# Memory columns on one engine, side evacuation one step earlier, and another order of the last projections in a segment-recurrent attention kernel

## The chip, the cores and the metric

One core of one Trainium2 chip. The metric is the device time of one execution in microseconds (us), lower is better. Before the change it was 822.22 us, the median of three runs (822.06 to 823.05). All runs told here were in the fast state; the granted TensorE clock was 0.996 to 1.000 in every one, so the clock explains none of the differences.

## The reference, cut to what matters

The input is one sequence of 2048 rows of 512. It is cut into 64 segments of 32 rows. Each segment is attended to together with 8 memory rows, and the memory of the next segment is the output of this one:

```python
mem = mem0
for s in range(n_seg):                                  # 64 segments
    h = jnp.concatenate([mem, xs], axis=1)              # 8 memory rows + 32 rows of x
    q, k, v = (einsum('btd,dhe->bhte', h, W) for W in (Wq, Wk, Wv))   # 32 heads of 128
    p = softmax(where(mask, q @ k.T * scale, -1e9))
    o = einsum('bhte,hed->btd', p @ v, Wo)
    mem = o[:, :M, :]                                   # recurrence
    outs.append(o[:, M:, :])
out = g * concat(outs) + (1 - g) * mlp(layernorm(x))
```
(written shorter than the original; the weights and the data are bfloat16.)

Only the 8 memory rows are needed to go on to the next segment. The kernel therefore takes "memory columns" out first, and does the output columns of a segment one or two steps later, beside the chain of the memory.

## The kernel before

One iteration of the loop is called a step; `s` is its number and `si = s % 4` its place in a tile of four. `bank(k)` is one of eight PSUM banks. A "side" job is work that isn't in the recurrence (keys, queries and values of the eight rows of a segment that don't fit beside the memory in a tile of 32 columns, and the output projection); it is done in small pieces where TensorE has room. Its copy out of PSUM is put in a queue and done by `flush`:

```python
def later(q, ev, k):            # queue a copy out of side bank k
    side_todo.add(k); q.append((k, ev))

def side(shape, dtype=FP32):    # hand out a side bank: whoever asks may have to empty it first
    side_n[0] += 1
    n = pools["nside"]
    while side_n[0] - n in side_todo:
        flush(dve_q)
        flush(act_q)
    return bank(5 + side_n[0] % n, shape, dtype)

def left_v(T, vb):              # V of the eight other rows: four matmul units, then
    ...
    def ev():
        vt = pools["sb"].tile([P, 4, Dh], BF16, tag="vt", bufs=1, name="vt")
        nc.scalar.copy(out=..., in_=bk[:])              # L282 in the profiles
        nc.sync.dma_start(vds[T][...], vt[...])         # L285, to DRAM and back to change the layout
    later(act_q, ev, side_k)
```

The loop, cut:

```python
for s in range(nseg):
    fill = side_work(T, si)
    ...
    if s >= 2:
        ux_out(s - 2)                     # output columns of two steps ago
        flush(act_q)
    ...
    flush(dve_q)
    for bi, (t, h0, h1) in enumerate(BANKS):            # q and k of the segment (L211),
        ...                                             # transposed on VectorE (L217), cast to QT, KT
    ...                                                 # V (L222), scores, exp
    nc.vector.reciprocal(out=R[...], in_=sm[:])         # L692, softmax sums of the memory rows
    ...                                                 # Pm = E * R (L695)
    Um = [bank(k, [P, NG, 8]) for k in (nd, ne, na, nc_)]
    av(Um, 8, s, V, Pm, 8, 0, 0)                        # P.V of the memory rows (L398, L403)
    sums(sr, ...)                                       # softmax sums of the other rows (L360)
    for j in range(4):                                  # the memory columns (L703)
        (nc.scalar.copy if j % 2 else nc.vector.tensor_copy)(out=UTT[Tp % 2][:, :, j, ...], in_=Um[j][:])
    nc.vector.reciprocal(out=R[:, 8 * NG:]..., in_=sr)  # L704, 1.76 us
    run_fill(1)
    flush(act_q, 2)
    for u in range(8):
        wo_unit(wp, UTT[Tp % 2], 24 - 8 * sp, u)        # Wo of the memory rows (L233); j = 0 first
    nc.scalar.copy(out=wsb[:], in_=wp[:])               # L711
    S_next = mask_mm()                                  # L374, in the bank of the sums
    if s >= 1:
        av_x(s - 1, ...)
    mem_out(aT, wsb)                                    # 16 small matmuls that turn the memory (L365)
    nc.vector.tensor_copy(out=hn[:, :, 0:M], in_=aT)    # hT, the next step's input (L721)
```

The four head groups j = 0 to 3 are copied by VectorE, ScalarE, VectorE, ScalarE. The tail after the last step does the output columns of the last three segments:

```python
    nc.gpsimd.tensor_tensor(out=racc[...], in0=racc[...], in1=Rl, op=ALU.add)
    ...
    wo_x(s - 2, nb, U1, 16)                             # matmuls and copy in one call
    ...                                                 # copies of U of step s - 1
    for _ in out_units(NT - 2):                         # output of the last but one tile
        flush(dve_q, 9)
    av_x(s, (nd, ne, na, nc_))
    wo_x(s - 1, nb, U1, 8)
    ...                                                 # copies of U of step s
    wo_x(s, 6, U0, 0)
    ...                                                 # projection of the left columns in two halves
    o_sb = cw.tile([P, Dm], BF16, tag="o", bufs=1, name="o")   # the same single buffer as in out_units
    for half in range(2):
        ...
        nc.vector.scalar_tensor_tensor(out=o_sb[:, d], ...)
        nc.sync.dma_start(out2[...], o_sb[:, d])
```

Of the kernel before, what the change touches and what calls it, by code (L numbers as in the profile page):

```python
# [11 lines left out]
ALU = mybir.AluOpType  # L12
# [11 lines left out]
def kernel(ctx, tc, A_x, A_mem0, A_Wq, A_Wk, A_Wv, A_Wo, A_seg_len, B_x, B_w1, B_b1, B_w2, B_b2, gate_w, out):  # L24
    nc = tc.nc
    P = 128
    _, S, Dm = A_x.shape
    H, Dh = A_Wq.shape[1], A_Wq.shape[2]
    M = A_mem0.shape[1]
# [5 lines left out]
    NT = S // P  # L35
# [3 lines left out]
    NG = H // 4  # L39
# [116 lines left out]
    for hh in range(4):  # L156
        for g in range(4):
            q = slice(32 * g, 32 * g + 32)
            for (c0, c1) in ((0, M), (EW - LEFT, EW)):
                sl = MkA[q, hh, c0:c1]  # L160
                nc.gpsimd.affine_select(out=sl, in_=sl, pattern=[[0, c1 - c0]], compare_op=ALU.is_ge,
                                        fill=MASK_NEG, base=-LEFT * hh, channel_multiplier=1)
            sl = MkA[q, hh, 0:M]
            nc.gpsimd.affine_select(out=sl, in_=sl, pattern=[[0, M]], compare_op=ALU.is_ge,
                                    fill=MASK_NEG, base=LEFT * hh + LEFT - 1, channel_multiplier=-1)
# [3 lines left out]
                                    fill=MASK_NEG, base=LEFT * hh, channel_multiplier=-1)  # L169
# [3 lines left out]
                                    fill=MASK_NEG, base=M, channel_multiplier=-1)  # L173
# [4 lines left out]
    def bank(k, shape, dtype=FP32):  # L178
        return pools["ps"].tile(shape, dtype, tag=f"b{k}", name=f"b{k}")

    side_n, side_todo = [0], set()
    dve_q, act_q = [], []

    def flush(q, n=1):
        for _ in range(min(n, len(q))):
            k, ev = q.pop(0)
            ev()
            side_todo.discard(k)

    def later(q, ev, k):  # L190
        side_todo.add(k)
        q.append((k, ev))

    def side(shape, dtype=FP32):
# [6 lines that stand above are left out]
# [29 lines left out]
    def wo_unit(bk, ut, c0, u, d0=0, d1=Dm):  # L230
        for (j, i) in HORD[4 * u:4 * u + 4]:
            g = i % 4
            nc.tensor.matmul(bk[32 * g:32 * g + 32, :], lhsT=ut[:, i, j, c0:c0 + 32], rhs=Wo_sb[:, 4 * i + j, d0:d1],  # L233
                             start=(j == 0 and i < 4), stop=(j == 3 and i >= NG - 4), tile_position=(0, 32 * g))
# [81 lines left out]
    def out_units(T):  # L316
        ob = side([P, Dm])
        side_k = side_n[0]
        for si in range(SPT):
            nc.tensor.matmul(ob[32 * si:32 * si + 32, :], lhsT=SelX[:], rhs=wsbs.pop(SPT * T + si + 2)[:], start=True, stop=False,  # L320
                             tile_position=(0, 32 * si))
        yield
        for si in range(SPT):
            nc.tensor.matmul(ob[32 * si:32 * si + 32, :], lhsT=SelL[si][:], rhs=wsbLs[T][:], start=False, stop=True,
                             tile_position=(0, 32 * si))

        def ev():
            o_sb = cw.tile([P, Dm], BF16, tag="o", bufs=1, name="o")
            nc.vector.scalar_tensor_tensor(out=o_sb[:], in0=ob[:], scalar=g_all[:, T:T + 1], in1=c_all[:, T, :], op0=ALU.mult, op1=ALU.add)
            nc.sync.dma_start(out2[T * P:(T + 1) * P, :], o_sb[:])  # L330
        later(dve_q, ev, side_k)
        yield

    def side_work(T, si):


        if si < 3 and T + 1 < NT:
            for n in range(2):
                if si == 0:
                    yield from left_v(T + 1, n)  # L340
                else:
                    yield from left_qk(T + 1, n, si - 1)
        if si == 3 and T >= 2:
            yield from out_units(T - 2)
        if si == 3 and T >= 1:
            yield from wo_left(T - 1)
# [45 lines left out]
    def av(U, n, s, V, Pt, c_main, c_left, u0):  # L392

        T, si = divmod(s, SPT)
        for i in range(NG):
            for j in range(4):
                q = slice(32 * j, 32 * j + 32)
                nc.tensor.matmul(U[j][:, i, :], lhsT=V[q, i, :], rhs=Pt[q, i, c_main:c_main + n],  # L398
                                 start=(i == 0), stop=False, skip_group_check=True, tile_position=(32 * j, 0))
        for g in range(2):  # L400
            for j in range(4):
                q = slice(32 * j, 32 * j + 32)
                nc.tensor.matmul(U[j][:, g:NG:2, u0:u0 + 8], lhsT=VL[T % 2][q, si, g, :], rhs=Pt[q, g:NG:2, c_left:c_left + 8],  # L403
                                 start=False, stop=True, skip_group_check=True, tile_position=(32 * j, 0))
# [188 lines left out]
    UTT = [lp.tile([P, NG, 4, 64], BF16, name=f"UTT{i}") for i in range(2)]  # L593
    racc = lp.tile([P, NG * 40], FP32)
# [15 lines left out]
    fill = iter(())  # L610
# [14 lines left out]
    def av_x(s, banks):  # L625
        U = [bank(k, [P, NG, 32]) for k in banks]
        av(U, 32, s, Vs.pop(s), Pxs.pop(s), 0, 32, 24)
        Uxs[s] = U
# [7 lines left out]
    for s in range(nseg):  # L636
# [3 lines left out]
        fill = side_work(T, si)  # L640
# [7 lines left out]
        na, nb, nc_, nd, ne = ring  # L648
        ring = (nb, nd, ne, na, nc_)
        qk_banks = (na, nb, nc_, nd, ne)  # L650
        if s >= 2:
            ux_out(s - 2)
            flush(act_q)
        if s + 1 < nseg:
            prep_h(s + 1)
        if s >= 1:
# [39 lines left out]
        Um = [bank(k, [P, NG, 8]) for k in (nd, ne, na, nc_)]  # L696
# [3 lines left out]
        sums(sr[:, :, 24:32], E[:, :, 48:56], False, True)  # L700
        Tp, sp = divmod(s - 2, SPT)
        for j in range(4):
            (nc.scalar.copy if j % 2 else nc.vector.tensor_copy)(out=UTT[Tp % 2][:, :, j, 24 - 8 * sp:24 - 8 * sp + M], in_=Um[j][:])  # L703
        nc.vector.reciprocal(out=R[:, 8 * NG:].rearrange("p (i q) -> p i q", q=32), in_=sr)  # L704
        run_fill(1)
        flush(act_q, 2)
# [1 line left out]
        wp = bank(nb, [P, Dm])  # L708
# [22 lines left out]
    Rl = R[:, 8 * NG:]  # L731
# [2 lines left out]
    Px = cw.tile([P, NG, 40], BF16, tag="Px", name="Px")  # L734
    nc.vector.tensor_tensor(out=Px[:, :, 0:32], in0=E[:, :, 16:48], in1=Rq, op=ALU.mult)
    nc.vector.tensor_tensor(out=Px[:, :, 32:40], in0=E[:, :, 48:56], in1=Rq[:, :, 24:32], op=ALU.mult)
    nc.gpsimd.tensor_tensor(out=racc[:, 8 * NG:], in0=racc[:, 8 * NG:], in1=Rl, op=ALU.add)
    Es.pop(s), Rs.pop(s)
    Pxs[s] = Px
    for _ in fill:  # L740
        pass
    flush(act_q, 9)

    def wo_x(sw, k, ut, c0):
        wp = bank(k, [P, Dm])
        for u in range(8):
            wo_unit(wp, ut, c0, u)
        wsb = cw.tile([P, Dm], BF16, tag="wsb", bufs=9, name="wsb")
        nc.scalar.copy(out=wsb[:], in_=wp[:])
        wsbs[sw + 2] = wsb  # L750

    U1, U0 = UTT[(NT - 1) % 2], UTT[NT % 2]
    wo_x(s - 2, nb, U1, 16)
    for j, U in enumerate(Uxs.pop(s - 1)):
        (nc.vector.tensor_copy if j % 2 else nc.scalar.copy)(out=U1[:, :, j, 8 + M:48], in_=U[:])
    for _ in out_units(NT - 2):
        flush(dve_q, 9)
    av_x(s, (nd, ne, na, nc_))
    wo_x(s - 1, nb, U1, 8)

    Ul = Uxs.pop(s)
    for j, U in enumerate(Ul):
        (nc.vector.tensor_copy if j % 2 else nc.scalar.copy)(out=U0[:, :, j, M:32], in_=U[:, :, 0:RIDE])  # L763
    for j, U in enumerate(Ul):
        (nc.vector.tensor_copy if j % 2 else nc.scalar.copy)(out=U1[:, :, j, 32:40], in_=U[:, :, RIDE:32])
    wo_x(s, 6, U0, 0)
    T = NT - 1
    HD2 = Dm // 2
    wL = cw.tile([P, Dm], BF16, tag="wsbL", bufs=1, name="wsbL")
    for half in range(2):  # L770
        d = slice(HD2 * half, HD2 * half + HD2)
        wp = bank((nc_, nd)[half], [P, HD2])
# [35 lines left out]
    with tc.If(n_bad > 0):  # L808
        with tc.tile_pool(name="gp", bufs=1) as gp, tc.tile_pool(name="gps", bufs=2, space=PSUM) as gps:
# [4 lines left out]
            def mem_tr():  # L814
                mp = gps.tile([P, KC, M], BF16, tag="m", name="mp")
                for kc in range(KC):
# [7 lines left out]
                                    fill=MASK_NEG, base=-M, channel_multiplier=1)  # L824
# [98 lines left out]
```

## Time and profile before

| what | before |
|---|---|
| time, median of 3 runs | 822.22 us |
| span of the profiled execution | 821.05 us |
| step 1, step 2 | 12.23, 10.82 us |
| median step with si = 0, 1, 2, 3 | 10.833, 10.779, 10.950, 11.439 us |
| from the last hT to the issue of the last output | 20.28 us |
| from that issue to the end | 4.29 us |

The step lengths are differences between the ends of successive casts of hT (L721) in the trace, with the first few and last steps left out of the medians. Because each step needs the hT of the one before, those four medians and the two end parts are the whole kernel, apart from the 112 us before the loop's first hT.

How to read the lines below: PE is TensorE's matmuls and PEld its weight loads, DVE is VectorE, ACT ScalarE, POOL GpSimd and SP SyncE, which issues the transfers; L703 is line 703 of the kernel of that run. A timeline line has the start in us, the time it took, engine, line of the program, operation, tile written and tile read, and in brackets how long the engine had been idle and what released it. A waits line has the waiting engine and tile, what it waited for, the sum in us, how often, and the longest. The wait that the first part of the change touches is this one, in the waits of the kernel before:

```profile
PEld L233 <- DVE UTT L703: 12.2, 63, 0.3
```

TensorE's weight load waits 63 times, 0.19 us each, for VectorE's copy of head group 0.

### The profile page before, as it was taken

Reading aid. Unit: us, or ns where it says so; the run is one execution under the profiler, and the core shown is the slowest. Engines: PE = TensorE matmul, PEld = TensorE weight load, DVE = VectorE, ACT = ScalarE, POOL = GpSimd, SP = SyncE. Lnnn points to the kernel's source line nnn. Section 1 sums busy time; section 2 is a strip of 40 time slices with the busy share of each in tenths; the row PEclk is TensorE's granted clock in tenths of the full one; section 3 lists DMA queues with packets and bytes.
Section 4 is the critical chain, followed back from the end, with each engine's and each line's share of the span. In section 5 each row is a group of like instructions: output and inputs, shape, how many; then the busy total and the mean of one; then the engine's idle time right before and its main releaser. Section 6 shows DMA issues by size and latency. Waiting matters only on the chain.

```text
span 821.1 us, 48437 instructions
## 1 busy us (share of the span) xinstructions
PE 793.0 (97%) x22013; PEld 443.4 (54%) x22013; DVE 493.1 (60%) x1022; ACT 446.6 (54%) x1239; POOL 272.7 (33%) x624
## 2 busy tenths in 40 slices
PE   6999999999999999999999999999999999999986
PEld 3666545555555555555555555555555555555543
DVE  5764256565656666665666565666566565756554
ACT  3555445655555555555555645555565555565553
POOL 8100224242434243243424242423333242424220
PEclk9999999999999999999999999999999999999999
DMA  9791310000000010101010100101010101010000
GB/s 314 238 404 48 104 28 11 25 16 15 25 20 26 10 36 10 37 11 33 6 38 10 31 17 20 27 18 28 10 36 11 36 4 40 7 34 8 10 5 24
DMA packets 38357, 37.59 MB, mean 46 GB/s; under 512 B 13561, under 2 KB 36578, under 8 KB 36610
## 3 DMA queue, kind: packets, MB, share of 16 engines
q1 hardware_dynamic: 38018, 34.31, 12.6%
q8 instruction: 174, 2.85, 1.5%
q14 instruction: 37, 0.30, 0.1%
q0 software_dynamic: 128, 0.13, 0.1%
HBM read 26.03 MB, written 6.29 MB: 39 GB/s over the span
## 4 chain that ended last, share of the span: by engine, by line
PE 92%; DVE 4%; issue 1%; DMA 1%; SPq 1%; ACT 1%; DVEq 0%; ACTq 0%
PE b L211 33%; PE b L233 18%; PE b L222 16%; PE b L398 5%; PE hp L470 4%; PE bp L487 4%; PE b L360 3%; PE b L374 2%; PE b L365 2%; PE b L383 2%; PE b L403 1%; DVE R L692 1%; DMA Wo_sb<-in_A_x_dram 1%; DVE Pm L695 1%; PE b L387 0%
## 5 line engine op out<-in xcount | busy, mean ns | idle before, releaser
L217 DVE STREAM_TRANSPOSE Tt<-b 128x512 f32<-128x512 f32 (+1 forms) x384 | 225.6, 613 | 82.2 <-PE b L211 70.3
L211 PEld LDWEIGHTS <-hT 128*32 128x32 bf16 x5120 | 131.3, 97 | 108.2 <-DVE hT L721 23.5
L233 PE MATMUL b<-Wo_sb,UTT 128*32 128x512 bf16 (+1 forms) x2656 | 160.9, 378 | 1.3 <-ACT UTT L763 0.9
L222 PE MATMUL b<-Wv_sb,hT 128*32 128x512 bf16 x2048 | 141.8, 378 | 0.0
L211 PE MATMUL b<-Wq_sb,hT 128*32 128x512 bf16 x2048 | 133.3, 380 | 3.2 <-DVE hT L721 1.7
L211 PE MATMUL b<-Wk_sb,hT 128*32 128x256 bf16 (+1 forms) x3072 | 133.3, 308 | 0.0
L667 ACT CAST KT<-Tt 128x256 bf16<-128x256 f32 (+1 forms) x192 | 87.1, 476 | 53.6 <-DVE Tt L217 53.5
L620 POOL TENSOR_TENSOR Px<-E,R 128x256 bf16<-128x256 bf16 x63 | 42.5, 675 | 208.9 <-DVE R L704 208.9
L704 DVE RECIPROCAL R<-b 128x256 f32<-128x256 f32 x63 | 110.7, 1757 | 0.0
L667 POOL CAST QT<-Tt 128x512 bf16<-128x512 f32 x64 | 39.2, 613 | 187.1 <-DVE Tt L217 187.1
L233 PEld LDWEIGHTS <-UTT 128*32 128x32 bf16 x2656 | 64.4, 96 | 63.8 <-DVE UTT L703 12.2
L711 ACT CAST wsb<-b 128x512 bf16<-128x512 f32 x63 | 36.9, 586 | 111.2 <-PE b L233 111.2
L692 DVE RECIPROCAL R<-b 128x64 f32<-128x64 f32 x63 | 35.1, 557 | 78.4 <-PE b L360 78.4
L634 ACT CAST UTT<-b 128x256 bf16<-128x256 f32 x248 | 74.4, 386 | 9.7 <-PE b L403 7.5
L667 ACT CAST QT<-Tt 128x512 bf16<-128x512 f32 x64 | 39.6, 619 | 68.7 <-DVE Tt L217 68.7
L222 PEld LDWEIGHTS <-hT 128*32 128x32 bf16 x2048 | 49.4, 96 | 21.2
L475 ACT ACTIVATE hg<-hp,b_sb 128x256 bf16<-128x256 f32 x80 | 37.8, 474 | 39.9 <-PE hp L470 39.9
L721 DVE CAST hT<-b 128x32 bf16<-128x32 f32 x63 | 12.1, 191 | 79.0 <-PE b L365 79.0
L398 PEld LDWEIGHTS <-V 32*128 32x128 bf16 x4064 | 34.4, 91 | 45.6 <-DVE Pm L695 32.3
L470 PE MATMUL hp<-yT,w_sb 128*128 128x256 bf16 (+1 forms) x352 | 54.7, 281 | 2.2 <-DMA w_sb<-in_B_w_dram 0.9
L703 ACT CAST UTT<-b 128x64 bf16<-128x64 f32 x126 | 20.6, 215 | 66.1 <-PE b L403 66.1
L622 POOL TENSOR_TENSOR racc<-racc,R 128x320 f32<-128x320 f32 x63 | 54.9, 871 | 0.0
(131 smaller groups left out, 1056.5 us busy)
## 6 DMA issues: line engine op xcount, KB each, us to landing
Wv_sb<-in_A_Wv_dram SPq DMA_DIRECT2D x4, 1024.0 KB
Wq_sb<-in_A_Wq_dram SPq DMA_DIRECT2D x4, 1024.0 KB
Wk_sb<-in_A_Wk_dram SPq DMA_DIRECT2D x4, 1024.0 KB
Wo_sb<-in_A_Wo_dram SPq DMA_DIRECT2D x2, 2048.0 KB
vd<-vt SPq DMA_DIRECT2D x32, 128.0 KB
vs<-vd SPq DMA_DIRECT2D x256, 16.0 KB
out_dram<-o SPq DMA_DIRECT2D x15, 128.0 KB
Wo_sb<-in_A_x_dram SPq DMA_DIRECT2D x1, 1024.0 KB
```

The costliest lines, as they stand in the source:

```text
L211: nc.tensor.matmul(bk[32 * j:32 * j + 32, 0:n], lhsT=G[:, kc, :], rhs=W5[t][:, kc, h0:h1, j, :], start=(kc == 0), stop=(kc == KC - 1), til ...
L217: nc.vector.transpose(out=Tt[:, 0:n], in_=bk[:, 0:n])
L222: nc.tensor.matmul(bk[32 * j:32 * j + 32, :], lhsT=G[:, kc, :], rhs=Wv5[:, kc, 4 * vb:4 * vb + 4, j, :], start=(kc == 0), stop=(kc == KC - ...
L233: nc.tensor.matmul(bk[32 * g:32 * g + 32, :], lhsT=ut[:, i, j, c0:c0 + 32], rhs=Wo_sb[:, 4 * i + j, d0:d1], start=(j == 0 and i < 4), stop ...
L398: nc.tensor.matmul(U[j][:, i, :], lhsT=V[q, i, :], rhs=Pt[q, i, c_main:c_main + n], start=(i == 0), stop=False, skip_group_check=True, til ...
L470: nc.tensor.matmul(hp[:rows, :], lhsT=w1_sb[:, kc, fc * P:fc * P + rows], rhs=yTs[blk][:, kc, :], start=(kc == 0), stop=(kc == KC - 1))
L620: nc.gpsimd.tensor_tensor(out=Px[:, :, 0:32], in0=E[:, :, 16:48], in1=Rr, op=ALU.mult)
L622: nc.gpsimd.tensor_tensor(out=racc[:], in0=racc[:], in1=R[:], op=ALU.add)
L634: nc.scalar.copy(out=UTT[T % 2][:, :, j, c0 + M:c0 + 40], in_=U[:])
L667: (nc.gpsimd.tensor_copy if bi == 2 else nc.scalar.copy)(out=dst, in_=Tv)
L692: nc.vector.reciprocal(out=R[:, 0:8 * NG].rearrange("p (i q) -> p i q", q=8), in_=sm[:])
L704: nc.vector.reciprocal(out=R[:, 8 * NG:].rearrange("p (i q) -> p i q", q=32), in_=sr)
```

## The change

The intent: take copies off VectorE, whose long reciprocal L704 follows them; take the transposition of a side job out of step 1's softmax chain by emptying the queue at the step's front; and order the tail so that a projection of finished columns fills each wait of TensorE.

```diff
@@ loop
         if s >= 2:
             ux_out(s - 2)
-            flush(act_q)
+        flush(act_q)
@@ memory columns
         for j in range(4):
-            (nc.scalar.copy if j % 2 else nc.vector.tensor_copy)(out=UTT[Tp % 2][:, :, j, ...], in_=Um[j][:])
+            nc.scalar.copy(out=UTT[Tp % 2][:, :, j, ...], in_=Um[j][:])
@@ tail
-    nc.gpsimd.tensor_tensor(out=racc[:, 8 * NG:], in0=racc[:, 8 * NG:], in1=Rl, op=ALU.add)
-    for _ in fill:
-        pass
-    flush(act_q, 9)
     def wo_x(sw, k, ut, c0):
         ...                              # matmuls
+        return sw, wp
+
+    def wo_x_out(sw, wp):                # the copy, now a call of its own
         wsb = cw.tile([P, Dm], BF16, tag="wsb", bufs=9, name="wsb")
         nc.scalar.copy(out=wsb[:], in_=wp[:])
         wsbs[sw + 2] = wsb
-    wo_x(s - 2, nb, U1, 16)
+    w61 = wo_x(s - 2, nb, U1, 16)
     ...                                  # copies of U of step s - 1
-    for _ in out_units(NT - 2):
+    wo_x_out(*w61)
+    for _ in fill:
         flush(dve_q, 9)
+    flush(act_q, 9)
     av_x(s, (nd, ne, na, nc_))
-    wo_x(s - 1, nb, U1, 8)
+    w62 = wo_x(s - 1, nb, U1, 8)
     ...                                  # copies of U of step s
-    wo_x(s, 6, U0, 0)
+    nc.vector.tensor_tensor(out=racc[:, 8 * NG:], in0=racc[:, 8 * NG:], in1=Rl, op=ALU.add)
+    wo_x_out(*w62)
+    w63 = wo_x(s, 6, U0, 0)
+    wo_x_out(*w63)
+    for _ in out_units(NT - 2):
+        flush(dve_q, 9)
```
(operands shortened where "..." stands.)

More of the change, by code (lines that the diff above doesn't have):

```diff
@@ L702 @@
         for j in range(4):
-            (nc.scalar.copy if j % 2 else nc.vector.tensor_copy)(out=UTT[Tp % 2][:, :, j, 24 - 8 * sp:24 - 8 * sp + M], in_=Um[j][:])
+            nc.scalar.copy(out=UTT[Tp % 2][:, :, j, 24 - 8 * sp:24 - 8 * sp + M], in_=Um[j][:])
         nc.vector.reciprocal(out=R[:, 8 * NG:].rearrange("p (i q) -> p i q", q=32), in_=sr)
```

## The prediction

> **What bounds the kernel now.** I read the engine totals first, then the chain that ended last, then the waits, then the timeline of single steps and of the last 20 us.
>
> ```profile
> PE 793.0 (97%) x22013; PEld 443.4 (54%) x22013; DVE 493.1 (60%) x1022; ACT 446.6 (54%) x1239; POOL 272.7 (33%) x624
> ...
> PE 92%; DVE 4%; issue 1%; DMA 1%; SPq 1%; ACT 1%; DVEq 0%; ACTq 0%
> ```
>
> TensorE is busy for 97% of the span and carries 92% of the chain, so VectorE and ScalarE have room, and taking work from either is worth nothing by itself. But the matmul ends are modelled, and each of the 64 steps is a recurrence: its memory columns must come out of PSUM, be projected by Wo, be copied, transposed into hT and fed to the next step's query. One middle step, in the timeline:
>
> ```profile
> 418.22 0.36 DVE L703 CAST UTT<-b 128x64 bf16<-128x64 f32 x2 [0.45 <-PE b L403]
> ...
> 418.25 0.33 ACT L703 CAST UTT<-b 128x64 bf16<-128x64 f32 x2 [0.96 <-PE b L403]
> ...
> 418.50 1.42 PEld L233 LDWEIGHTS <-UTT 128*32 128x32 bf16 x32 [0.19 <-DVE UTT L703]
> 418.50 1.91 PE L233 MATMUL b<-Wo_sb,UTT 128*32 128x512 bf16 x32
> 418.53 1.76 DVE L704 RECIPROCAL R<-b 128x256 f32<-128x256 f32 x1
> ...
> 420.46 0.59 ACT L711 CAST wsb<-b 128x512 bf16<-128x512 f32 x1 [1.39 <-PE b L233]
> ```
>
> The weight load of the Wo projection waits for the first VectorE copy (418.22 plus 0.22 is 418.44; 0.06 later TensorE starts). This wait totals 12.2 us over 63 steps. Only head group 0 is needed to start; each later group is needed 0.43 us after the one before it (32 matmuls of Wo in 1.74 us, four groups). After Wo come wsb (0.59), its transposition and hT.
>
> Two places hold real waste. Step 1:
>
> ```profile
> 118.08 0.61 ACT L282 CAST vt<-b 128x512 bf16<-128x512 f32 x1
> 118.58 0.72 DVE L217 STREAM_TRANSPOSE Tt<-b 128x512 f32<-128x512 f32 x1 [2.49 <-PE b L211]
> ...
> 119.22 0.52 DVE L692 RECIPROCAL R<-b 128x64 f32<-128x64 f32 x1
> ...
> 120.12 0.36 PE L398 MATMUL b<-Pm,V 32*128 32x8 bf16 x32 [0.99 <-DVE Pm L695]
> ```
>
> The softmax reciprocal stands behind a side transposition. Its sums end at 117.59, so it could start at 117.65. The tail:
>
> ```profile
> 807.90 0.40 PE L320 MATMUL b<-wsb,SelX 128*32 128x512 bf16 x4 [1.19 <-DVE bad L804]
> ...
> 811.66 3.66 PE L233 MATMUL b<-Wo_sb,UTT 128*32 128x512 bf16 x96 [0.91 <-ACT UTT L763]
> ```
>
> TensorE stands still 1.19 us and then 0.91 us.
>
> [...] medians 219 (VectorE) and 216 ns (ScalarE). [...] the last step's L736 took 0.75 us with GpSimd's L737 running, against 0.22 us for a multiplication of the same shape in L695. [...] here, from SyncE, an output issued at 807.88 let VectorE go at 809.72, 1.84 us later.
>
> **The change part by part.**
>
> *Memory columns on ScalarE alone.* Removes 126 VectorE copies of 219 ns, adds 126 on ScalarE. ScalarE is idle there (0.96 us before its copy). Its copies start about 0.11 us apart, so four end within 0.6 us, and the second head group is needed only 0.43 us after Wo starts: groups 1 to 3 never wait. What counts is the first. ScalarE's first copy now starts 0.03 us after VectorE's, of which some 0.01 us is that its matmul ends one place later; I take 0.025 us later, with a duration about 0.012 us shorter (single rows 213 against 225 ns). The release costs are alike (copy of wsb ends, 0.05 us, next weight load). Net: Wo starts 0.013 us later. In three of four steps this chain sets the step (TensorE reaches the transposition of wsb with no slack), 47 steps: **+0.6 us**. In every fourth step side matmuls stand before the transposition, and it costs 0. The freed VectorE buys nothing: the long reciprocal L704 waits for the sums of TensorE, which end at 418.40, not for the copies; and all steps need its end only for the mask. Step 0, where VectorE's copy was late (108.40 after ScalarE's 108.37), gains 0.06.
>
> *Side evacuation from the second step on.* From step 2 the call already ran; only step 1 changes. There the pending vt copy goes to the front of the step, so asking for a side bank no longer forces the two queues, and the transposition moves to the next step, as it does in all later ones. Casts of hT stand at 111.62, 123.86, 134.68 in steps 0 to 2 and at 156.33, 167.11, 178.06 in steps 4 to 6: two steps take 23.06 against 21.73 us. **-1.3 us**. Once, not 63 times.
>
> *Order of the last projections.* The same matmuls, re-ordered; I walk it forward with the durations of before. The first projection of the tail now stands right after the sums but writes the bank that V's second half is copied from (802.24 to 802.83), so it starts at 802.88 and not 802.65: a new wait of 0.2 us. 1.73 for it, 0.43 for the out matmuls, 1.73 for the left projection: 806.77. The last attention product finds its Px ready ([...] the second multiplication 0.2 instead of 0.75, done by 805.3). 0.38 later the second projection, 807.15 to 808.89; the third follows with no gap, its copies done by 808.0: to 810.62. So 0.91 is gone. Then the check matmul and out matmuls of the last but one tile; these share the bank of the third projection, whose copy runs 810.85 to 811.44. New wait: TensorE goes on at 811.49, 0.85 idle. Final halves start 811.92 (before: 813.39), 1.47 earlier.
> But the final output uses the one `o` buffer. The output DMA before it now leaves only at 812.9 (before: 810.49), and lands 1.7 to 1.8 later, 814.65; VectorE would be ready at 814.3. The final o starts at about 814.8 against 815.78. **-1.0 us**.
>
> Sum: -1.3 - 0.06 + 0.6 - 1.0 = -1.8, so 822.2 - 1.8 = **820.4 us**.
>
> **Rivals.**
> (a) *ScalarE serializes.* Four copies in a row delay Wo by one copy each step, 0.1 us times 47 = +5 us, to 825. For it: they are in a row. Against: only group 0 gates the start. If PE waited for all four, Wo would start 0.3 us later, +14.
> (b) *VectorE relief pays.* If L704 started earlier by the 0.06 us that separates it from the copies' end, the mask would start earlier: at most 0.06 in each of the 15 full fourth steps, -0.9 us, and up to -3.8 over all. Against: an L704 waiting for the sums gains nothing, and wsb gates three steps of four.
> (c) *The tail moves its wait.* Both new waits (bank of the third projection, the one `o` buffer) could take all: if the DMA landed at 815.5 the tail gives 0 and the time is 821.5. Against: landing times are steady near 1.7 us. Without the `o` wait, -1.5, 819.9.
> (d) *ScalarE's start is not later.* Then the +0.6 is gone: 819.8; if it is 0.03 later, 821.3.
>
> **Range and chances.** The separate uncertainties: steady state -0.9 to +1.6 us, step 1 -1.0 to -1.5, tail -0.4 to -1.5, and the runs of before lie 1.0 us apart. I choose 818.9 to 821.7. A 2% change is 16.4 us, nine times the sum: within 2% is nearly sure.
>
> **What will show it.** In the profile after: four ScalarE copies at the memory columns, the wait for them at the Wo weight load 12 to 14 us in total (right), or 15 and more (rival a); L704 at the same 0.03 us after Wo's start (right) or earlier (rival b); step 1 near 10.8 us with L217 gone from between the sums and L692; in the tail no wait on the UTT copies, instead one of about 0.8 us at the out matmuls for ScalarE's wsb, and VectorE's last o waiting for a DMA. The prediction is wrong if ordinary steps differ by more than 0.03 us, which 47 repetitions would turn into more than 1.4 us, or if the final matmuls don't come earlier.

## The result, and the profile after

| | runs | median | range |
|---|---|---|---|
| before, same chip | 4 | 822.63 us | 822.06 to 823.24 |
| after | 4 | 820.66 us | 819.82 to 822.00 |

The ratio is 0.9977, 95% interval 0.9960 to 0.9995. A ratio here is the mean time of one kernel's fast runs over the mean of the other's fast runs of the same rounds, so it isn't quite the ratio of the two medians. The change gains about 1.9 us, 0.23%: the same within 2%, and 0.26 us from the predicted 820.4.

The engine totals and the chain that ended last, on the page of the kernel after:

```profile
PE 791.7 (97%) x22013; PEld 443.6 (54%) x22013; DVE 473.6 (58%) x897; ACT 461.8 (56%) x1365; POOL 271.4 (33%) x623
...
PE 93%; DVE 2%; DMA 1%; SPq 1%; issue 1%; ACT 1%; DVEq 0%; ACTq 0%
```

126 instructions have moved from VectorE to ScalarE (1022 to 897 and 1239 to 1365; the one VectorE instruction that this leaves over is the racc addition from GpSimd). VectorE is busy 19.5 us less, and the chain doesn't care: TensorE still carries it.

The middle step that the prediction showed, in the timeline of the kernel after:

```profile
417.40 0.56 ACT L703 CAST UTT<-b 128x64 bf16<-128x64 f32 x4 [0.92 <-PE b L403]
...
417.66 1.42 PEld L233 LDWEIGHTS <-UTT 128*32 128x32 bf16 x32 [0.17 <-ACT UTT L703]
...
417.71 1.76 DVE L704 RECIPROCAL R<-b 128x256 f32<-128x256 f32 x1 [0.76 <-PE b L360]
417.82 0.63 ACT L282 CAST vt<-b 128x512 bf16<-128x512 f32 x1
```

Four copies on ScalarE end within 0.56 us, and Wo's first weight load starts 0.26 us after the first of them starts (0.28 before). The idle time before it is 0.17 (0.19 before). L704 starts 0.05 us after Wo, and here the profile names TensorE's sums (L360) as what released it. In 60 of the 63 steps it names ScalarE's copy instead (the first line below). I still read L704 as waiting for the sums, because its start hasn't moved against them: the median is 0.093 us after their end in both kernels. In this step there is also something that the prediction didn't look at: the side copy L282, which sends a transfer off, now stands behind all four copies. In the waits of the kernel after:

```profile
DVE R L704 <- ACT UTT L703: 46.8, 60, 1.0
...
PEld L233 <- ACT UTT L703: 11.1, 63, 0.3
```

Step 1 in the timeline of the kernel after:

```profile
112.13 0.58 ACT L282 CAST vt<-b 128x512 bf16<-128x512 f32 x1 [0.86 <-PE b L222]
...
117.70 0.56 DVE L692 RECIPROCAL R<-b 128x64 f32<-128x64 f32 x1 [1.58 <-PE b L360]
...
118.65 0.36 PE L398 MATMUL b<-Pm,V 32*128 32x8 bf16 x32
...
122.48 0.70 DVE L217 STREAM_TRANSPOSE Tt<-b 128x512 f32<-128x512 f32 x1
```

The vt copy has gone from 118.08 to 112.13, the reciprocal follows the sums at once (117.70, before 119.22), and the side transposition has moved behind the next hT, to 122.48.

The tail, first TensorE, VectorE and ScalarE up to the last halves, then VectorE's last o, in the timeline of the kernel after:

```profile
801.84 1.41 PEld L233 LDWEIGHTS <-UTT 128*32 128x32 bf16 x31 [0.16 <-issue]
...
803.98 0.22 DVE L736 TENSOR_TENSOR Px<-E,R 128x64 bf16<-128x64 bf16 x1
...
810.54 0.40 PE L320 MATMUL b<-wsb,SelX 128*32 128x512 bf16 x4 [0.69 <-ACT wsb L748]
...
810.98 1.28 PE L233 MATMUL b<-Wo_sb,UTT 128*32 128x256 bf16 x40
...
815.48 0.88 DVE L794 SCALAR_TENSOR_TENSOR o<-b,g_all,c_all 128x256 bf16<-128x256 f32 x2 [2.04 <-DMA out_dram<-o]
```

The predicted new waits are there: 0.16 us where V's bank was predicted (the profile names no releaser, but ScalarE's copy of V ends at 801.78, 0.05 us before Wo's first matmul), 0.69 at the out matmuls, and the last o behind an output transfer, 2.04. The final matmuls start at 810.98, 2.4 us earlier than before; 1.05 of that comes from the steps.

Where the time of the traces went, from the same reading as in the table of before:

| part | before | after | after, second trace |
|---|---|---|---|
| steps 1 and 2 | 23.05 | 21.65 | 21.66 |
| steps 3 to 62 | 661.62 | 661.93 | 661.63 |
| median step, si = 0, 1, 2, 3 | 10.833, 10.779, 10.950, 11.439 | 10.890, 10.771, 10.945, 11.441 | 10.898, 10.771, 10.945, 11.444 |
| last hT to last output issue | 20.28 | 20.99 | 20.90 |
| that issue to the end | 4.29 | 3.82 | 3.92 |
| span | 821.05 | 820.24 | 820.09 |

Two cautions belong here. In the kernel after, the si = 0 steps fall in two groups, near 10.82 and near 10.96 us, and their median lies in the gap between them; the means of all fifteen (10.842 before, 10.905 and 10.916 after) say the same, 0.06 to 0.07 us more. And in both sessions the profiled execution of the changed kernel was its slowest (822.00 and 821.93, against medians of 820.66 and 820.92). So the traces show 0.8 and 1.0 us of gain where the times show 1.9. About 1 us of the difference lies in executions that left no trace.

### The profile page after: what moved, and what is told of

The parts are those of the page before. It is cut to its first block, busy times and chain, and to the rows that moved or that the text cites. A ratio compares the mean times of both kernels' runs of the same rounds, so it can differ in the third digit from the quotient of the medians.

```text
span 820.2 us, 48440 instructions
## 1 busy us (share of the span) xinstructions
PE 791.7 (97%) x22013; PEld 443.6 (54%) x22013; DVE 473.6 (58%) x897; ACT 461.8 (56%) x1365; POOL 271.4 (33%) x623
## 4 chain that ended last, share of the span: by engine, by line
PE 93%; DVE 2%; DMA 1%; SPq 1%; issue 1%; ACT 1%; DVEq 0%; ACTq 0%
PE b L211 34%; PE b L233 17%; PE b L222 17%; PE b L398 5%; PE hp L470 4%; PE bp L487 4%; PE b L360 3%; PE b L374 2%; PE b L383 2%; PE b L365 2%; PE b L403 1%; DMA Wo_sb<-in_A_x_dram 1%; PE b L387 0%; DVE R L692 0%; DVE hT L721 0%
## 5 line engine op out<-in xcount | busy, mean ns | idle before, releaser
L704 DVE RECIPROCAL R<-b 128x256 f32<-128x256 f32 x63 | 110.7, 1757 | 49.3 <-ACT UTT L703 46.8
L233 PEld LDWEIGHTS <-UTT 128*32 128x32 bf16 x2656 | 64.8, 96 | 61.2 <-ACT UTT L703 11.1
L703 ACT CAST UTT<-b 128x64 bf16<-128x64 f32 x252 | 35.3, 227 | 63.1 <-PE b L403 63.1
```

The costliest lines, as they stand in the source:

```text
L233: nc.tensor.matmul(bk[32 * g:32 * g + 32, :], lhsT=ut[:, i, j, c0:c0 + 32], rhs=Wo_sb[:, 4 * i + j, d0:d1], start=(j == 0 and i < 4), stop ...
L704: nc.vector.reciprocal(out=R[:, 8 * NG:].rearrange("p (i q) -> p i q", q=32), in_=sr)
```

## The experiments

Eleven kernels; all results were correct. The first theory was the prediction's own sum. After the trace of the changed kernel there were two more questions: why some si = 0 steps had become some 0.13 us longer (theory: the side transfer of vt now lands later, rival: ScalarE's row of copies itself), and why the output transfer in the tail took so long.

| kernel | runs | median (range) | before | ratio (95%) | steps 3-62 | last hT to last issue | to the end |
|---|---|---|---|---|---|---|---|
| e1_copies | 5 | 823.16 (822.44-823.44) | 822.82 | 1.0004 (0.9990-1.0018) | 661.45 | 20.28 | 4.95 |
| e2_flush | 5 | 820.13 (820.00-821.17) | 822.82 | 0.9971 (0.9957-0.9985) | 660.42 | 20.28 | 4.36 |
| e3_tail | 5 | 821.91 (821.55-823.48) | 822.82 | 0.9995 (0.9981-1.0009) | 661.62 | 20.13 | 3.84 |
| e4_swap | 5 | 819.43 (818.92-820.55) | 822.82 | 0.9962 (0.9948-0.9976) | 660.12 | 20.50 | 3.72 |
| e5_obuf | 5 | 820.50 (819.23-821.17) | 823.42 | 0.9961 (0.9948-0.9974) | 662.00 | 19.18 | 4.35 |
| e6_bank | 5 | 821.56 (821.09-821.88) | 823.42 | 0.9977 (0.9965-0.9990) | 661.48 | 19.44 | 5.28 |
| e7_vt | 6 | 827.53 (824.34-828.56) | 823.42 | 1.0047 (1.0031-1.0063) | 664.99 | | |
| e8_dve | 4 | 832.60 (831.89-833.08) | 823.42 | 1.0110 (1.0095-1.0124) | 673.41 | | |
| after2 | 5 | 820.92 (820.53-821.93) | 822.80 | 0.9977 (0.9963-0.9990) | 661.63 | 20.90 | 3.92 |
| e9_swapo | 5 | 819.40 (818.07-819.92) | 822.80 | 0.9955 (0.9941-0.9968) | 660.22 | 18.91 | 4.90 |
| e10_all | 5 | 819.04 (817.97-820.13) | 822.80 | 0.9952 (0.9938-0.9965) | 661.16 | 18.05 | 5.74 |

The last column moves by 2 us between kernels whose last transfers are the same two. In eleven of the thirteen traces SyncE's wait for these transfers ends 2.4 to 3.5 us after the last issue. In e6 and e10 it ends by 2.25, and there the program's end waits for TensorE instead. After the kernel's check of its own sums, every engine reads the flag `bad` (made in L810 of the changed kernel) and branches on it; TensorE's branch takes 3.36 to 4.04 us in all thirteen traces, those of the other engines at most 0.08. In e6 and e10 VectorE makes the flag only behind the last o, so SyncE stands still for TensorE's branch for 2.06 and 2.56 us. In before, e1, e2 and e9 it does so for 0.2 to 0.3. That alone makes single traces unfit to settle half a microsecond of the tail.

### One part at a time

**e1_copies**: the kernel before with the copies alone.

```diff
-            (nc.scalar.copy if j % 2 else nc.vector.tensor_copy)(out=UTT[Tp % 2]...
+            nc.scalar.copy(out=UTT[Tp % 2]...
```

> The kernel before with the memory columns copied by ScalarE alone. Theory now (from the profile after): ScalarE's first copy starts no later than VectorE's did and is 0.012 us shorter, so Wo starts 0.016 us earlier in every step and chain-bound steps are 0.01 us shorter, 47 of them: -0.5 us; but the side V copy stands behind four copies, its DMA is issued 0.2 us later and lands while the memory transposition ends, and some steps of the first kind of each four are 0.13 us longer (8 of 15 in the profile after: +1.0 us). Sum about +0.5 us (0 to +1). The prediction's step said +0.6 with Wo 0.013 us later in every step. Rival (four copies in a row delay Wo): +5 us.

Measured: 823.16 against 822.82, ratio 1.0004, so no more than a few tenths of a microsecond either way can be read. The rival that ScalarE's row costs a copy in each step (+5 us) is out: the interval's upper end is +1.5 us. The long si = 0 steps are there: seven steps have the extra wait, 0.81 us in all (one step of another kind, step 7, has a small one in every kernel and isn't counted here or below).

**e2_flush**: the kernel before with the flush alone.

```diff
         if s >= 2:
             ux_out(s - 2)
-            flush(act_q)
+        flush(act_q)
```

> The kernel before with the side evacuation at the front of step 1 alone. Theory: step 1 shrinks from 12.23 to 10.8 us, step 2 grows by 0.1, all else as before: -1.3 us. Rival (the effect of it is given back by later side work): 0.

Measured: 820.13, ratio 0.9971, -2.4 us, more than the whole change gives; the interval reaches from -1.2 to -3.5, so the expected -1.3 is only just in it. In the trace steps 1 and 2 take 21.67 instead of 23.05 (-1.38, as expected). Steps 3 to 62 are 1.20 shorter, though their medians are equal to before's within 0.004 us in all four kinds: the difference is in single steps, most of it in steps 21, 34, 35 and 42, which are 0.24 to 0.35 us longer than their kind in the trace of before and not here. What those are is taken up below.

**e3_tail**: the kernel before with the tail alone.

```diff
 (the changed kernel with the first two hunks of the change undone)
```

> The kernel before with the new order of the last projections alone. Theory: the last Wo matmuls end 1.4 us earlier, but the last o waits for the landing of the output DMA before it (one o buffer); with a landing of 1.6 us as 15 of 16 parts of it had in the profile after: -1.0 us; with the late part of that profile (3.4 us): +0.5 us. Expect -0.2 to -1.0 and a wider spread of the runs than before's. Rival (the wait for the bank of the third projection takes all): 0 with no DMA wait in the profile.

Measured: 821.91, ratio 0.9995 (0.9981 to 1.0009), inconclusive in time. The trace has the last issue 0.15 us sooner after the last hT and the end 0.45 us sooner after that; of the second, 0.2 us is TensorE's branch, which the end waits for in before and not here. The last o waited 1.18 us for the output transfer.

### What the copies do to a step

**e4_swap**: the changed kernel with groups 0 and 2 on ScalarE, 1 and 3 on VectorE, that is the split of before with the engines exchanged.

```diff
-            nc.scalar.copy(out=UTT[Tp % 2]...
+            (nc.vector.tensor_copy if j % 2 else nc.scalar.copy)(out=UTT[Tp % 2]...
```

> The kernel after with head groups 0 and 2 on ScalarE and 1 and 3 on VectorE. If what moved Wo is who copies the first group: Wo starts as in after (0.51 us after the last attention matmul), and the side V copy is issued 0.2 us earlier again, so the 0.13 us delays of the first step of each four vanish: about 1 us below after. If Wo moved because VectorE was relieved: Wo at 0.527 as before. If the delays come from elsewhere than the timing of the side DMA: as after within 0.3 us.

Measured: 819.43, ratio 0.9962. A middle step in its timeline:

```profile
416.22 0.33 ACT L703 CAST UTT<-b 128x64 bf16<-128x64 f32 x2 [0.92 <-PE b L403]
416.26 0.36 DVE L703 CAST UTT<-b 128x64 bf16<-128x64 f32 x2 [0.48 <-PE b L403]
416.44 0.60 ACT L282 CAST vt<-b 128x512 bf16<-128x512 f32 x1
416.49 1.42 PEld L233 LDWEIGHTS <-UTT 128*32 128x32 bf16 x32 [0.17 <-ACT UTT L703]
```

Wo starts as early as in the changed kernel (0.17 idle), because group 0 is on ScalarE: its copies take 0.212 us against 0.225 (the first of each group, in the traces of after and before), and ScalarE starts no later than VectorE did (0.065 against 0.068 us after the end of the attention matmul before it). The side copy L282 starts 0.05 us before Wo; in the changed kernel it starts 0.16 after (417.82 against 417.66). And the long si = 0 steps are gone: one step with the extra wait (48, which before has too) instead of seven, the si = 0 median 10.822 instead of 10.890. The ratio is 0.0015 below that of the changed kernel, but their intervals overlap, so it is the steps that decide here and not the time. Here are a long and an ordinary si = 0 step of the changed kernel, first step 24, then step 28, where the memory's small matmuls end and hT is cast:

```profile
376.16 0.26 PE L365 MATMUL b<-Sel,wsb 128*32 128x8 bf16 x16
376.43 1.20 ACT L634 CAST UTT<-b 128x256 bf16<-128x256 f32 x4 [0.33 <-PE b L365]
376.63 0.19 DVE L721 CAST hT<-b 128x32 bf16<-128x32 f32 x1 [1.28 <-PE b L365]
...
420.27 0.27 PE L365 MATMUL b<-Sel,wsb 128*32 128x8 bf16 x16
...
420.61 0.19 DVE L721 CAST hT<-b 128x32 bf16<-128x32 f32 x1 [1.14 <-PE b L365]
```

In both the cast's start is set by L365; it comes 0.21 us after L365's end (376.42 to 376.63) in step 24 and 0.07 in step 28. In step 24 ScalarE too gets its release later than usual. In the seven long steps hT starts 0.13 to 0.25 us after L365's end, in the median step 0.09. What lies there is not the side transfer itself but the one queued behind it on SyncE, the load of input rows `xT`. In the timeline of the kernel after, step 28:

```profile
418.48 0.34 SPq L285 DMA_DIRECT2D vd<-vt  x1
418.91 2.80 SPq L241 DMA_TRANSPOSE xT<-in_A_x_dram  x2
```

In step 24 the 16 packets of 4 bytes that end the transfer of vt are over 0.44 us before L365 starts. Those that end the load of xT lie 0.14 to 0.29 us after L365's end, the last of them 0.56 us after its start. It is much the same in the other six long steps. In the ordinary step 28 they come at 0.55 to 0.70, when hT has long been let go. In e4 both transfers leave 0.23 us earlier, and in six steps these packets are over 0.06 us after L365's end, in time. In the traces of all kernels but e8 (where every step waits longer) there are 34 si = 0 steps with 0.1 us or more of extra wait; 33 of them have 20 or more of these packets in or across the time from 0.08 to 0.26 us after L365's end, against 28 of the other 146, and 19 of those 28 are steps 4 and 32, in most of which L365 itself is stopped (below). So it is shown that the two meet, and that the delay goes when the transfers go earlier (e4). Why the release of VectorE and ScalarE comes later then is not shown.

**e8_dve**: the changed kernel with all four copies on VectorE, the mirror of the change.

```diff
-            nc.scalar.copy(out=UTT[Tp % 2]...
+            nc.vector.tensor_copy(out=UTT[Tp % 2]...
```

> The kernel after with all four memory copies on VectorE. Theory: Wo starts as in the kernel before (0.527 us), so the copies themselves cost nothing, but the long reciprocal starts some 0.29 us later, the mask matmul waits for it, and the attention product and the memory transposition behind it come 0.2 to 0.3 us later in each step: +12 to +18 us. Rival (the reciprocal has slack): +1 us or less.

Measured: 832.60, ratio 1.0110, 9.2 us above the kernel before, less than expected, but by the expected mechanism. A middle step in its timeline:

```profile
421.95 0.62 DVE L703 CAST UTT<-b 128x64 bf16<-128x64 f32 x4 [0.45 <-PE b L403]
422.22 1.42 PEld L233 LDWEIGHTS <-UTT 128*32 128x32 bf16 x32 [0.18 <-DVE UTT L703]
...
422.48 1.75 DVE L704 RECIPROCAL R<-b 128x256 f32<-128x256 f32 x1
```

Wo starts as before, since group 0 is still done first. But L704 stands behind the four copies and starts 0.26 us after Wo instead of 0.05. The next mask is written into the bank that L704 reads, so it comes 0.21 us later, behind it the memory's transposition 0.15, and a median step is 0.20 to 0.28 us longer than before. So VectorE's load at this place does matter, in one direction only: two copies were free, four are not.

**e7_vt**: the changed kernel with the side copy behind the copy of wsb, to move the side transfer later by about 2 us.

```diff
         run_fill(1)
-        flush(act_q, 2)
         wsb = ...
         nc.scalar.copy(out=wsb[:], in_=wp[:])
+        flush(act_q, 2)
```

> The kernel after with the side V copy behind the copy of wsb instead of behind the memory columns. Theory: its DMA then lands in the next step's projections, the 0.13 us pauses between the memory transposition and the cast of hT in the first step of each four vanish (0.25 down to 0.08 us in 8 steps): -1.0 us against after. Rival (the pauses have nothing to do with that DMA): the same number of them, time as after; a cost of the move itself (ScalarE late for the next step's casts) would show as longer waits for QT.

Measured: 827.53, ratio 1.0047, a miss. The six runs fall in two groups (824.3 to 825.0 and 826.9 to 828.6), and the traced one, 824.97, is of the lower, so some 3 us of the upper group have no trace. What the theory said of the long steps came true: no si = 0 step with the extra wait, and their median 10.822. But the move makes other waits, in the waits of this kernel:

```profile
PEld L383 <- ACT KT L667: 14.6, 60, 1.0
ACT vt L282 <- DMA vd<-vt: 12.7, 10, 3.1
```

`vt` has one buffer. The second copy of a pair now finds the first one's transfer still on its way, ScalarE stands for up to 3.1 us with the casts of KT behind it, and TensorE's scores wait for those. So earlier and later transfers both cure the extra wait, and only the earlier one costs nothing. And ScalarE's row of four copies, which this kernel keeps, is not what makes the long steps.

### The tail

**e5_obuf**: the changed kernel with a buffer of its own for the last o.

```diff
-    o_sb = cw.tile([P, Dm], BF16, tag="o", bufs=1, name="o")
+    o_sb = cw.tile([P, Dm], BF16, tag="oL", bufs=1, name="oL")
```

> The kernel after with a buffer of its own for the last output tile. Theory: the last o no longer waits for the landing of the output DMA before it (2.04 us of waiting in the profile after, where one of 16 parts of that DMA landed 1.7 us late; some 0.4 us where none is late): -0.4 to -2.0 us against after, with a narrower spread of the runs, and no DMA wait before the last o in the profile. Rival (the end is set by the last matmuls): 0.

Measured: 820.50, ratio 0.9961 against 0.9977 for the changed kernel. It was run at another time. The last o in its timeline:

```profile
813.79 0.96 DVE L794 SCALAR_TENSOR_TENSOR oL<-b,g_all,c_all 128x256 bf16<-128x256 f32 x2
```

No wait; the last issue comes 19.18 us after the last hT instead of 20.99, so 1.8 us hung on that buffer. In time about 1.3 us of it seems to be left (the difference of the ratios, 0.0016 of 823); the two intervals overlap, so the wait is shown to be gone and its worth isn't measured closely.

**e6_bank**: the changed kernel with the third projection and the check's matmul in banks of their own.

```diff
-    w63 = wo_x(s, 6, U0, 0)
+    w63 = wo_x(s, 5, U0, 0)
...
-    cnt = side([1, 1])
+    cnt = bank(7, [1, 1])
```

> The kernel after with the third projection of the tail in PSUM bank 5 and the check matmul in bank 7. Theory: the out matmuls of the last but one tile no longer wait 0.7 to 0.85 us for the copy of the third projection; everything after them, the output DMA included, is 0.75 us earlier: -0.75 us against after. Rival (the late DMA sets the end): the matmuls are earlier but the time is the same within 0.3 us.

Measured: 821.56, ratio 0.9977, the same as the changed kernel, as the rival said; but the late transfer is only half of the reason. The out matmuls don't wait for ScalarE any more and the last issue comes 1.55 us earlier, but the last o in its timeline still waits for the transfer, and the end of the program comes 5.28 us after the last issue (3.82 in the changed kernel):

```profile
813.56 0.88 DVE L794 SCALAR_TENSOR_TENSOR o<-b,g_all,c_all 128x256 bf16<-128x256 f32 x2 [1.35 <-DMA out_dram<-o]
...
814.35 0.13 DVE L810 TENSOR_SCALAR bad<-b 1x1 int32<-1x1 f32 x1
```

The second line is the other half. The edit also moved the check: its flag is made at 814.35, behind the last o, where the changed kernel made it at 809.94, behind the third projection. TensorE's branch therefore ends 4.2 us after the last issue, and the end waits for it. So this run doesn't test the bank of the third projection alone.

**after2**: the changed kernel again.

> The changed kernel once more, unchanged, to have its time and its trace on the same chip as the next two. If the delays of 0.13 to 0.15 us in every fourth step belong to the schedule, seven to nine steps have them again, at the same step numbers, and the sum of extra lag lies at 0.9 to 1.4 us; if they are chance, other steps or far fewer. If the late last part of the output transfer belongs to two transfers in flight, the last VectorE o waits again 1.3 to 2.1 us; if it was chance, below 0.8 us. Time about 2.0 us below the kernel before (ratio 0.9965 to 0.9985).

Measured: 820.92, ratio 0.9977. Seven steps with the extra wait, 0.86 us in all, slightly under the range; five of them (16, 24, 40, 44, 52) are the same as in the first trace. So the delays belong to the schedule, though not every one keeps its step. The last o waited 1.96 us again, so the late transfer isn't chance either.

**Why the transfer is late.** The output leaves as 128 packets of 1 KB and 16 of 4 bytes. The view of the transfers, for 811.9 to 815.6 us of the kernel after, from its issue on (the first line is the busy tenths in 40 slices, the second the GB/s, then packets, MB and share for each queue):

```profile
DMA  0000000009799730000000201000000000600000
GB/s 0 0 0 0 0 0 0 0 0 188 266 321 332 277 111 11 0 0 0 0 0 0 89 0 11 0 11 11 11 11 11 22 0 0 177 0 0 0 0 0
...
q1 hardware_dynamic: 144, 0.13, 10.8%
q8 instruction: 2, 0.03, 4.0%
```

The same view, for 810.4 to 812.5 us of the kernel before, of the transfer at that place (issued at 810.49; its buffer too is taken over by the last o, but nothing has to wait):

```profile
DMA  0000000000000000025899998510000000000000
```

In the kernel after, most of it is done by 813.33, 1.35 us after the issue, and then a thin rest of 11 GB/s runs until 814.91. In the packets' times this rest is nine packets: eight of 1 KB and one of 4 bytes, one sixteenth of the transfer. The semaphore of this transfer has 16 updates in the trace: 15 from 813.50 to 813.69 and the last at 815.36, 3.37 us after the issue; the last o starts at 815.48, so VectorE went on only after the sixteenth. For the transfer at that place in the kernel before the 16 updates come 1.52 to 1.71 us after the issue. The first late packet starts at 814.15, and a 16 KB packet of the instruction queue q8 runs from 812.77 to 814.16. I looked at this output transfer, the last but one to be waited for, in all traces: in after, after2 and e3 to e10 such a 16 KB packet lies over it, exactly nine packets are late, the first starts within 0.02 us of that packet's end, and the last ends 2.07 to 2.92 us after the issue. In before, e1 and e2 such a packet is over 0.06 to 0.55 us after the issue, before the first data moves at 0.83, and the last ends after 1.35 to 1.36. Ten of ten and three of three, and in the ten the landing follows the packet: it comes 0.65 to 0.74 us after the packet's end, which varies from 1.42 to 2.18. So the reading is that such an instruction packet holds one part of the output up, and that the new order of the tail, which all ten have, brings the two together. How it does so isn't shown: the trace doesn't say which DMA engine moved a packet. No run moved the instruction packet alone, so this is not an experiment. But the traces hold far more cases than this one. Each has 15 output transfers of 128 KB, 195 in all. In 124 of them no such packet lies over the data, and they end 1.35 to 1.52 us after the issue. The other 71 end after 1.57 us or more, up to 3.6, and in every one a late data packet starts within 0.03 us of the end of a 16 KB instruction packet. Three of the 15 in the kernel before are of this kind (issued at 279.10, 367.49 and 588.43; they end after 2.28 to 2.90 us), so it could have been seen before the change.

### The stops in the recurrence

The 16 matmuls of L365 take 0.27 us. In some steps they stop in their middle, with no wait recorded, as here in the timeline of the kernel after:

```profile
265.00 0.21 PE L365 MATMUL b<-Sel,wsb 128*32 128x8 bf16 x8
265.63 0.21 PE L365 MATMUL b<-Sel,wsb 128*32 128x8 bf16 x8 [0.41 <-issue]
```

In 13 traces 34 of the 819 strings of L365 are longer by more than 0.1 us in this way (by 0.40 and 0.55 in before, by 0.24, 0.57 and 0.58 in after), all in steps 4, 9, 14 and 32. Every stop ends 1.23 to 1.52 us after the end of a 16 KB packet of the instruction queue q8, and after an interval of 4.7 to 6.4 us between that packet and the one before it, where the median interval is 4.2 us. Of the 785 strings without a stop 110 (14%) have the end of a packet at that distance, and 34 of them after such an interval too. So a late packet goes with every stop, but not every late packet makes one. q8 carried 174 packets of 16,384 bytes, and TensorE did 44,026 matmuls and weight loads, 253 for each packet. That q8 brings TensorE its instructions, and that TensorE stops for want of them, is my reading of the count and of the stops: the trace doesn't say which engine a packet is for. Why a packet is late in one step and not in another is open. And not all stops are of this kind. In steps 21, 34, 35 and 42 of the kernel before TensorE's matmuls and signals are on time, and another engine starts late: VectorE with a transposition in 21, 35 and 42, ScalarE with the exponential in 34. Steps 21 and 34 in the timeline of the kernel before:

```profile
337.46 0.45 DVE L217 STREAM_TRANSPOSE Tt<-b 128x256 f32<-128x256 f32 x1 [0.25 <-issue]
...
481.93 0.28 ACT L685 ACTIVATE E<-b 128x128 bf16<-128x128 f32 x1 [0.26 <-issue]
```

In step 35 VectorE passes its wait for TensorE at the same moment as in step 39, which is of its kind, and starts the transposition 0.35 us later than there. These four steps are late in e3 too, by the same amounts within 0.01 us, and in none of the other eleven traces; step 47 is late by 0.48 to 0.49 us in after, after2, e5, e6 and e7 alone. So they belong to the program and not to chance. In each of these steps a packet of 8 KB of another instruction queue, q14, ends 1.4 to 2.6 us after the late start. Such a packet lies in 40% of all steps, so this points at instruction packets again but doesn't prove it.

### Both cures together

**e9_swapo**: the changed kernel with the split of e4 and the buffer of e5.

```diff
-            nc.scalar.copy(out=UTT[Tp % 2]...
+            (nc.vector.tensor_copy if j % 2 else nc.scalar.copy)(out=UTT[Tp % 2]...
...
-    o_sb = cw.tile([P, Dm], BF16, tag="o", bufs=1, name="o")
+    o_sb = cw.tile([P, Dm], BF16, tag="oL", bufs=1, name="oL")
```

> The changed kernel with groups 0 and 2 of the memory columns copied by ScalarE and 1 and 3 by VectorE, and with a buffer of its own for the last o. If the two savings are separate (earlier side transfers, no wait for the output transfer), they add: 1.2 + 1.2 us below the changed kernel, about 4.3 us below the kernel before, ratio 0.9940 to 0.9956; no more than three steps with the extra lag, no DMA wait ahead of the last o, tail 23.4 to 23.8 us. If the saving of one was only a slow or a fast spell of the other's runs, the ratio is no better than 0.9960.

Measured: 819.40, ratio 0.9955, at the edge of the expected range: 1.5 us below the changed kernel of the same call, where 2.4 was expected. That is only 0.0006 to 0.0007 below the ratios of e4 and e5, well inside their intervals, so it isn't shown that the two savings add; the rival's 0.9960 lies inside the interval of this run too. Two long steps, the last o without a wait (oL at 811.73), the last issue 18.91 us after the last hT. The end comes 4.90 us after that issue, 1.0 more than in the changed kernel. So part of the tail's gain is given back after the last issue. SyncE's wait for the last transfers ends 3.46 us after it (2.58 in the changed kernel), with a 16 KB instruction packet over them once more, from 0.80 to 2.42 us after the issue, and then 0.2 us are spent on TensorE's branch.

**e10_all**: the same with the banks of e6.

> The same with the third tail projection and the check matmul in other banks. With the output transfer out of the way the matmuls that come 0.7 us earlier should now reach the end: 0.5 to 0.7 us below the version without the other banks, tail 22.8 to 23.2 us, ratio 0.9933 to 0.9950. Rival: the wait moves to ScalarE's copies of the last projection or to the landing of the two last transfers, and the times are equal within 0.2 us.

Measured: 819.04, ratio 0.9952. The last issue comes another 0.86 us earlier (18.05) and the end another 0.84 later (5.74), so the two versions are the same within what can be read. The wait did move on, as the rival said, but to neither of the two places that it named: the outputs are in by 2.20 us after the last issue, and the end waits for TensorE's branch until 4.76. Both beat the kernel before by 3.4 to 3.8 us and the changed one by 1.5 to 1.9.

## Why the prediction was right or wrong

The time, 820.66, was inside the range, and the sum of -1.8 met the measured -1.9. Term by term it is less good: two terms hold, one was right in its sum and wrong in its reason, and one was mis-sized. That the sum still fits is luck, as the last point shows.

- **What bounds, and what the freed VectorE buys (nothing): right.** L704 still starts 0.093 us after TensorE's sums, and the totals moved 19.5 us between the engines without moving the chain. e8 shows that the reserve at that place is small: two copies more and it is the bound.
- **Memory columns, +0.6 us over 47 steps, from Wo 0.013 us later in each: the reason was wrong.** ScalarE's first copy starts no later than VectorE's did, and takes 0.013 us less. Measured from the attention's last matmul Wo starts 0.016 us earlier, and si = 1 and si = 2 steps are 0.008 and 0.005 us shorter: this was the prediction's own rival (d). What it left out is that ScalarE has the side copy behind these four, and that the load of xT, queued behind the transfer that this sends, then ends just when the memory's small matmuls do. Medians of si = 0 steps are 0.057 us longer, which fails the prediction's own test (ordinary steps no more than 0.03 us apart; the other three kinds pass it); 15 of them are +0.86; with the others, 60 steps at their medians come to 660.71 against 660.01, +0.7. The predicted +0.6 was met by a cost of another kind.
- **Step 0, -0.06: not seen**; the first hT ends 0.04 us later than before, and as its end lies anywhere from 111.46 to 112.21 us in the thirteen traces, 0.06 us can't be read there.
- **The rival of ScalarE serializing: rejected as argued**, by e1 and by the wait of 11.1 us where it needed 15 and more (the prediction's own 12 to 14 was slightly high, since Wo came earlier).
- **Side evacuation, -1.3 us once: right.** -1.40 in the trace, -1.38 in e2 alone. e2's further 1.2 us are mostly the four late starts of VectorE and ScalarE, 1.3 us in all, that the traces of before and e3 have and e2's hasn't. They come with the program, but nobody predicted them.
- **Tail, -1.0 us: mis-sized, and the failed step is "lands 1.7 to 1.8 later".** The walk up to there held: 0.16 for the bank of V (0.2 predicted), L736 in 0.22 us (0.2; the 0.75 of before stood beside GpSimd's L737, which is gone, but no run changed that alone), 0.69 at the out matmuls (0.85), the final halves 1.36 us earlier when the steps' 1.05 is taken off (1.47), the output transfer issued at 811.99, which is 813.04 on the old clock (812.9). But VectorE was let go 3.37 us after the issue, so the last o came 1.7 us later than predicted. From the last hT to the last issue the tail is 0.7 us longer than before, instead of 1.0 shorter. Rival (c), "the one o buffer could take all", was the truth; the argument against it, "landing times are steady near 1.7 us", rested on transfers with no instruction packet over them; three of the fifteen in the trace of before already took 2.3 us and more to the last data packet, and 2.77 to 3.36 to the last of the 16 updates, where the other twelve took 1.71 to 2.00.
- **The two errors and the stops cancel in the traces, and not quite.** By the first trace: 0.04 before step 1, -1.40 in steps 1 and 2, +0.7 in the medians, -0.4 in stops and other odd steps, +0.7 and -0.5 in the tail, -0.8 in all. The times say -1.9. The rest, about 1 us, stays open, since the profiled executions were slow ones.

## What to carry to other kernels

When a copy moves to another engine, look at what stands behind it on that engine's queue, above all a copy that starts a transfer: 0.2 us more ahead of it cost more here (0.81 us in seven long steps of e1) than the copy itself gained (0.008 and 0.005 us in the steps with si = 1 and 2). A single buffer between two output transfers made the slowest of 16 parts a wait of 2.04 us for the last instruction here, so give the last output its own; and then look at what else the end waits for, here a branch. And when single parts are worth a microsecond in 800, test them alone and several times: the smallest one-line part (e2) gained as much as the whole, and half of that came from steps that it was not meant to touch.
